# Block products for FFN2: seven instead of eight in half of the batches

## The chip, the core and the metric

The kernel runs on one core of a Trainium2 chip. A core has five engines with queues of their own: TensorE (PE: matrix products from SBUF into PSUM; its weight loads are listed as PEld), VectorE (DVE), ScalarE (ACT), GpSimd (POOL) and SyncE (SP). Each works through its own queue in order and waits only for the data, or the space, that the next instruction needs. DMA queues move data between HBM and SBUF. The metric is the device time of one execution in microseconds, lower is better.

## The reference

The inputs are q, k, v (8 batches, 8 heads, 576 tokens, 64 features), phi (the same with 32 memory slots) and four weight matrices.

```python
a = softmax(phi, axis=2)                       # over the 32 slots
k_m = einsum('bhsm,bhsd->bhmd', a, k)          # 32 slot keys per head, v_m alike
attn = softmax(q @ k_m.T / 8) @ v_m            # over the 32 slots
x = attn with the 8 heads side by side         # 4608 tokens x 512
h = max(x @ w1, x @ w2, x @ w3)                # 4608 x 768
out = h @ w_out                                # 4608 x 512, float32
```

(The softmax lines stand for an exponential divided by its sum; the reference subtracts the maximum first and adds 1e-9 to the sum.)

## The kernel before

Tokens of a batch lie so that 128 partitions hold pairs of heads. The product with v_m is never formed: x @ w = attn @ (v_m @ w), and the small v_m @ w ("fold") is made for each batch. Since max(x w1, x w2, x w3) = max(x (w1 - w3), x (w2 - w3), 0) + x w3, the hidden layer hT holds max(relu(attn wp1), attn wp2), six tiles of 128 features by the tokens of two batches, and the part x w3 w_out is added in FFN2 as attn times a folded matrix wp3 (256 slots by 512). So FFN2 of 128 tokens is eight matmuls into one PSUM bank: six hT tiles against w_out (wo_sb, L497) and two attn tiles against wp3 (L506), with 512 columns each.

The whole kernel is an order written out by hand at its end: a list of pieces, `letter number @ batch`, issued one after another. Each piece puts its instructions into the queues of its engines, so the list sets the order within every engine. A "!" moves a piece's work to the other engine (`swap`). The pieces:

- L0 to L3: load phi, k, v, q of a batch (L93, L97, L110), all from GpSimd's queue. Buffers: two batches of each. H and Y: the same for batch 0 and the weights.
- E: exponential of phi on ScalarE. r0, r1: GpSimd packs k and v into one tile kvr (`pack`, L103), from batch 2 on.
- B: the slot keys and values, 72 small matmuls over the packed k, v and a column of ones (`att_kv`, L249). N: their division by the sums on VectorE. K: transposes on TensorE and a copy. Q0, Q1: transposes of q on VectorE (`att_q`, L313).
- S: the scores and their exponential (`att_score`, L333 and L342). a, s, c: VectorE transposes, sums over the slots, reciprocals. m: the product with the reciprocals, on GpSimd (`att_mul`, L409). X: transposed back into attn (L417).
- D0 to D3: folds of v_m into w1, w2, w3 w_out (`fold`, L440, copied out at L172 or L176). F0 to F11: FFN1, one tile of features for one of the two weight differences (`ffn1`, L466); the even ones are copied with a relu (L170), the odd ones are joined by a maximum on VectorE (L479).
- T0 to T4: FFN2, 128 tokens each (`ffn2`, L497, L506). A batch of 576 tokens has four tiles of 128 and 64 tokens over; T4 of an odd batch joins the two remainders (L515). The copy from PSUM is on ScalarE for nearly all of them (L172), and SyncE writes the tile out (L527). T3 of batch 7, the last piece, is done in two halves of 256 columns (`ffn2_last`, L538, L546) with the copies on VectorE (L555) and ScalarE (L558).
- W, O, V: once, at the start: w3 transposed (into w3T), w3 w_out, and the differences w1 - w3, w2 - w3 (`w_diff`, L213). Z: warm-up matmuls.

PSUM has eight banks. A second string, `banks`, gives the bank of every piece in the order of issue; F, S, B and D take a pair, T and K one.

## Time and profile before

| | us |
|---|---|
| median of 3 timed runs | 164.94 (164.56 to 165.78) |
| span of the profiled execution, first to last instruction | 163.3 |
| end of its last matmul | 159.6 |
| TensorE busy | 153.8 (94%) |
| ScalarE busy | 100.6 (62%) |
| VectorE busy | 90.4 (55%) |
| GpSimd busy, issuing of DMAs included | 69.5 (43%) |

"Busy" is the time in which at least one instruction of the engine runs. A matmul's row gives its time from start to modelled end, which overlaps with the next; what a stream of matmuls costs is read from the distances of their starts, or from the chain that ended last. The page cuts the span into 40 slices of 4.08 us and gives busy shares as digits (9 is 90% or more). In a group's row come the line, engine and operation, the tiles written and read, their shapes and the count; behind the first bar the busy time and the mean of one in ns; behind the second the engine's idle time ahead of it and what ended most of that.

### The profile page before, as it was taken

To read this page: it belongs to the slowest core of one execution; us is meant where nothing else is said; L and a number is where in the kernel's file an instruction comes from. 1 tells how busy PE (TensorE), PEld (TensorE's weight loads), DVE (VectorE), ACT (ScalarE), POOL (GpSimd) and SP (SyncE) were. 2 spreads that over 40 slices of the span, in tenths; PEclk is the share of its full clock that TensorE was granted. 3 is DMA by queue.
4 is the path that set the end of the run, shared out by engine and by line. 5 is a ranking of instruction groups with operands and counts; after the bars stand their busy time and mean duration, and the time that the engine had idled before them with its cause. 6 is when DMAs were issued, how large, how long until landed. Compare 5 with 4: busy or idle time off the path is not lost.

```text
span 163.3 us, 4838 instructions
## 1 busy us (share of the span) xinstructions
PE 153.8 (94%) x2080; PEld 85.3 (52%) x2080; DVE 90.4 (55%) x181; ACT 100.6 (62%) x151; POOL 69.5 (43%) x71
## 2 busy tenths in 40 slices
PE   7978798899899999999999999999999999999990
PEld 2433444564377436743673575576553468744450
DVE  2023704798838665849399748879749128810010
ACT  4205445845497488778885899994658976223320
POOL 7932205100599259657968957646403100000000
PEclk9999999999999999999999999999999999999998
DMA  6999999999999999999999999996313130014333
GB/s 150 152 206 207 205 210 217 274 208 210 253 313 238 209 253 379 274 210 293 252 263 206 232 355 264 191 233 150 130 69 129 69 128 0 0 68 186 135 128 130
DMA packets 21974, 31.77 MB, mean 195 GB/s; under 512 B 1216, under 2 KB 16576, under 8 KB 21952
## 3 DMA queue, kind: packets, MB, share of 16 engines
q0 software_dynamic: 16080, 21.43, 68.7%
q1 hardware_dynamic: 5728, 9.90, 17.2%
q8 instruction: 16, 0.26, 0.6%
q10 hardware_dynamic: 144, 0.13, 0.2%
q14 instruction: 6, 0.05, 0.1%
HBM read 39.32 MB, written 9.44 MB: 299 GB/s over the span
## 4 chain that ended last, share of the span: by engine, by line
PE 83%; DMA 9%; POOL 2%; ACT 2%; issue 1%; DVE 1%; ACTq 0%; POOLq 0%
PE psum L497 29%; PE psum L466 28%; DMA wo_sb<-in_moe_w_out_dram 9%; PE psum L506 8%; PE psum L440 6%; PE psum L249 4%; PE psum L192 3%; PE psum L333 2%; PE psum L515 1%; ACT h L170 1%; PE psum L538 1%; PE psum L298 1%; POOL kvo L97 1%; ACT wp L172 1%; POOL qq L110 0%
## 5 line engine op out<-in xcount | busy, mean ns | idle before, releaser
L497 PE MATMUL psum<-wo_sb,hT 128*128 128x512 bf16 x210 | 51.3, 380 | 0.0
L466 PE MATMUL psum<-attn,wp 128*128 128x288 bf16 x384 | 50.5, 286 | 0.1
L479 DVE TENSOR_TENSOR hT<-psum,h 128x576 bf16<-128x576 f32 x48 | 34.2, 749 | 18.0 <-PE psum L466 12.5
L466 PEld LDWEIGHTS <-wp 128*128 128x128 bf16 x384 | 36.7, 98 | 13.2 <-issue 2.0
L172 ACT COPY ot<-psum 128x512 f32<-128x512 f32 x35 | 20.7, 591 | 32.1 <-PE psum L506 25.2
L497 PEld LDWEIGHTS <-hT 128*128 128x128 bf16 x210 | 19.2, 97 | 24.0 <-issue 4.3
L172 ACT CAST wp<-psum 128x1024 bf16<-128x1024 f32 (+1 forms) x31 | 29.2, 995 | 3.8 <-PE psum L440 2.0
L103 POOL COPY kvr<-kvo 128x2304 bf16<-128x2304 bf16 x12 | 25.3, 2111 | 13.7 <-DMA kvo<-in_k_dram 10.1
L170 ACT ACTIVATE h<-psum 128x576 bf16<-128x576 f32 x47 | 28.4, 659 | 3.5 <-PE psum L466 3.3
L409 POOL TENSOR_TENSOR t<-t,sm 128x576 bf16<-128x576 bf16 x14 | 16.1, 1154 | 24.6 <-DVE sm L404 24.4
L506 PE MATMUL psum<-wp,attn 128*128 128x512 bf16 x62 | 18.4, 379 | 0.0
L159 PE MATMUL psum<-warm 128*128 128x512 bf16 x44 | 12.1, 427 | 1.2 <-DVE warm L128 1.2
L313 DVE STREAM_TRANSPOSE qT<-qq 128x576 f32<-128x576 f32 x16 | 11.7, 747 | 1.4 <-DMA qq<-in_q_dram 1.4
L342 ACT ACTIVATE e<-psum 128x576 bf16<-128x576 f32 x16 | 9.6, 652 | 3.8 <-PE psum L333 3.8
L229 ACT ACTIVATE e<-ph 128x1152 bf16<-128x1152 f32 (+1 forms) x9 | 9.6, 1065 | 1.7 <-DMA ph<-in_phi_dram 1.6
L395 DVE TENSOR_REDUCE sm<-t 128x18 f32<-128x576 bf16 x14 | 10.3, 738 | 0.2
L387 DVE STREAM_TRANSPOSE t<-e 128x288 f32<-128x288 f32 x14 | 6.4, 465 | 6.2 <-ACT e L342 6.1
L97 POOL DMA_DIRECT2D kvo<-in_v_dram x9 | 6.7, 749 | 7.1 <-PE psum L249 4.1
L506 PEld LDWEIGHTS <-attn 128*128 128x128 bf16 x62 | 6.1, 98 | 7.1
L110 POOL DMA_DIRECT2D qq<-in_q_dram x8 | 6.2, 770 | 6.6 <-DVE h L174 3.7
L555 DVE COPY ot<-psum 128x256 f32<-128x256 f32 x1 | 0.4, 425 | 15.4 <-PE psum L546 15.4
L249 PEld LDWEIGHTS <-e 64*32 64x32 bf16 x720 | 6.9, 90 | 3.7 <-issue 3.3
(57 smaller groups left out, 114.4 us busy)
## 6 DMA issues: line engine op xcount, KB each, us to landing
out_dram<-ot SPq DMA_DIRECT2D x35, 256.0 KB, 5.6
qq<-in_q_dram POOLq DMA_DIRECT2D x8, 576.0 KB, 12.2
ph<-in_phi_dram POOLq DMA_DIRECT2D x7, 576.0 KB, 14.4
kvo<-in_k_dram POOLq DMA_DIRECT2D x7, 576.0 KB, 14.6
kvo<-in_v_dram POOLq DMA_DIRECT2D x7, 576.0 KB, 15.6
w_sb<-in_moe_w_dram POOLq DMA_DIRECT2D x3, 768.0 KB, 19.0
wo_sb<-in_moe_w_out_dram POOLq DMA_DIRECT2D x1, 768.0 KB, 14.6
ph<-in_phi_dram SPq DMA_DIRECT2D x2, 288.0 KB, 3.0
```

What stands on the lines that cost most here:

```text
L103: nc.gpsimd.tensor_copy(out=kvrs[b % 2][:, :, :, D * i : D * (i + 1)], in_=kvos[b % 2][:, 1 - i])
L159: nc.tensor.matmul(po[:, 0:BANK], lhsT=warm[:, 0:P], rhs=warm, start=True, stop=True)
L170: nc.scalar.activation(out=out_, in_=in_, func=AF.Relu)
L172: nc.scalar.copy(out=out_, in_=in_)
L249: nc.tensor.matmul(kvp[M * j : M * (j + 1), a, 0:nd], lhsT=s["e"][r, j, c, :], rhs={None: lambda: kvr[r, j, c, 0:nd], 0: lambda: k_and_one ...
L313: nc.vector.transpose(out=s["qT"][:, j].rearrange("p j c r e -> p (j c r e)").bitcast(FP32), in_=loaded[b]["q"][:, j].rearrange("p j c d - ...
L395: nc.vector.tensor_reduce(out=sm, in_=s["t", g].rearrange("p n r e -> p n e r"), op=ALU.add, axis=mybir.AxisListType.X,)
L409: nc.gpsimd.tensor_tensor(out=t, in0=t, in1=s["sm", g].unsqueeze(2).to_broadcast([P, S // HP, R, 2]), op=ALU.mult,)
L466: nc.tensor.matmul(acc[:, h, 0:SH], lhsT=wps[b][:, g, w * DF + ft * P : w * DF + (ft + 1) * P], rhs=attn[:, g, c0 : c0 + SH], start=(g == ...
L479: nc.vector.tensor_tensor(out=hT[:, ft, (b % 2) * S : (b % 2 + 1) * S].rearrange("p (h n) -> p h n", h=2), in0=a, in1=s["h1", ft], op=ALU.max,
L497: nc.tensor.matmul(po, lhsT=hT[:, fc, c0 : c0 + P], rhs=wo_sb[:, fc, :], start=(n == 0), stop=False,)
L506: nc.tensor.matmul(po, lhsT=attn[:, g, c0 : c0 + P], rhs=wp3s[b][:, g, :], start=False, stop=(g == NG - 1),)
```

## The change

FFN2 of batches 3, 4, 5 and 6 (512 of their 576 tokens; the 64 left over stay in T4) is done by seven products of half blocks instead of eight. The product of tokens by 1024 "features" (six hT and two attn tiles) and of 1024 by 512 is cut into two by two blocks each: tokens in two interleaved halves of 256 (r), features in two halves (three hT tiles and one attn tile each), output columns in two halves of 256. Sums and differences of blocks are formed first:

- U0 to U3: of the weights. For w_out once (batch number 9), 768 elements a partition each, on GpSimd, into the space of w3T; for wp3 of each batch, 256 elements each.
- A0 to A3: of the hT blocks, 768 elements each; A4 to A7: of the attn blocks, 256 each. A2 overwrites the block of hT it reads.
- P0 to P6: the products, eight matmuls of 256 columns each. They share three banks a batch: x for P1, P4, P5, P6, y for P0 and P3, z for P2. Partial sums are copied out of a bank while it goes on accumulating (after P0, P1 and P4); three additions on VectorE and one copy give the output, which is written out after P4 and P6, 512 KB each.

A and U run on GpSimd or VectorE according to "!" (U!: VectorE; A!: GpSimd). Five softmax products m (m1@1, m1@2, m0@2, m1@3, m1@4) go to VectorE. The list of pieces and the bank string are new, opool has four buffers instead of six, and for batches 0 and 1 the tile with k and v begins with the ones, which lie ahead of k and v now. The bank string is left out below.

```diff
-    opool = ctx.enter_context(tc.tile_pool(name="opool", bufs=6))
+    opool = ctx.enter_context(tc.tile_pool(name="opool", bufs=4))
-    def att_mul(b, g):
+    def att_mul(b, g, swap):
-        nc.gpsimd.tensor_tensor(
+        (nc.vector if swap else nc.gpsimd).tensor_tensor(
...
+    KT = FT // 2
+    CH = DM // 2
+    TW = 2 * P
+    SUB, ADD = ALU.subtract, ALU.add
+    B11, B12, B21, B22 = [
+        (slice(KT * i, KT * (i + 1)), slice(CH * j, CH * (j + 1)))
+        for i in range(2)
+        for j in range(2)
+    ]
+    tw = w3T.rearrange("p f j n -> p (f j n)").rearrange("p (i k c) -> p i k c", i=4, k=KT)
+    sa0 = const.tile([P, 4, TW], BF16, name="sa0")
+    oj0 = [const.tile([P, 2, DM], FP32, name=f"oj{i}") for i in range(2)]
+    SNAP = {0: "m5", 1: "m1", 4: "u2"}
+    twb, sas, quads = {}, {}, {}
+    def combine(on_dve, out_, in0, in1, op):
+        eng = nc.vector if on_dve else nc.gpsimd
+        eng.tensor_tensor(out=out_, in0=in0, in1=in1, op=op)
+    def combine_w(b, i, on_dve):
+        if b == B + 1:
+            x = {n: wo_sb[:, n[0], n[1]] for n in (B11, B12, B21, B22)}
+            t = [tw[:, n] for n in range(4)]
+        else:
+            if b not in twb:
+                twb[b] = work.tile([P, 4, CH], BF16, name="twb")
+            w = wp3s[b]
+            x = {n: w[:, n[0].start // KT, n[1]] for n in (B11, B12, B21, B22)}
+            t = [twb[b][:, n] for n in range(4)]
+        in0, in1 = [(x[B12], x[B11]), (x[B22], t[0]), (x[B22], x[B12]), (x[B21], t[1])][i]
+        combine(on_dve, t[i], in0, in1, SUB)
+    def sums(b):
+        if b not in sas:
+            if b == B - 1:
+                s = inp.tile([P, NP, NC, D], BF16, name="sx", tag="qq")
+                s = s.rearrange("p j c d -> p (j c d)").rearrange("p (i n) -> p i n", i=3)
+                sa = inp.tile([P, NP, NC, D], BF16, name="sy", tag="qq")
+                sa = sa.rearrange("p j c d -> p (j c d)")[:, 0 : 4 * TW]
+                sa = sa.rearrange("p (i n) -> p i n", i=4)
+            else:
+                s, sa = w_sb[:, 0:3, 2], sa0
+            sas[b] = (
+                s.rearrange("p i (k q n) -> p i k q n", k=KT, q=2),
+                sa.rearrange("p i (q n) -> p i q n", q=2),
+            )
+        return sas[b]
+    def blocks(x, b, k):
+        c0 = (b % 2) * (S + HP)
+        x = x[:, :, c0 : c0 + 2 * TW]
+        return [
+            [
+                x[:, k * i : k * (i + 1)].rearrange("p f (q r n) -> p f q r n", q=2, r=2)[
+                    :, :, :, r
+                ]
+                for i in range(2)
+            ]
+            for r in range(2)
+        ]
+    def combine_a(b, i, on_dve):
+        s, sa = sums(b)
+        n = i % 4
+        if i < 4:
+            (a11, a12), (a21, a22) = blocks(hts[b // 2], b, KT)
+            t = {0: s[:, 0], 1: s[:, 1], 2: a21, 3: s[:, 2]}
+        else:
+            (a11, a12), (a21, a22) = blocks(attns[b // 2], b, 1)
+            t = {m: sa[:, m : m + 1] for m in range(4)}
+        in0, in1 = [(a21, a22), (t[0], a11), (a11, a21), (a12, t[1])][n]
+        combine(on_dve, t[n], in0, in1, ADD if n == 0 else SUB)
+    def products(b, i, swap):
+        s, sa = sums(b)
+        h, a = blocks(hts[b // 2], b, KT), blocks(attns[b // 2], b, 1)
+        wp3 = wp3s[b]
+        def plain(r, c):
+            return lambda k, q: h[r][c][:, k, q] if k < KT else a[r][c][:, 0, q]
+        def summed(n):
+            src = h[1][0] if n == 2 else s[:, min(n, 2)]
+            return lambda k, q: src[:, k, q] if k < KT else sa[:, n, q]
+        def w_plain(i, j):
+            c = slice(CH * j, CH * (j + 1))
+            return lambda k: wo_sb[:, KT * i + k, c] if k < KT else wp3[:, i, c]
+        def w_summed(n):
+            return lambda k: tw[:, n, k] if k < KT else twb[b][:, n]
+        lhs, rhs, name = [
+            (summed(0), w_summed(0), "y"),
+            (plain(0, 0), w_plain(0, 0), "x"),
+            (plain(0, 1), w_plain(1, 0), "z"),
+            (summed(3), w_plain(1, 1), "y"),
+            (summed(1), w_summed(1), "x"),
+            (summed(2), w_summed(2), "x"),
+            (plain(1, 1), w_summed(3), "x"),
+        ][i]
+        acc = quads.setdefault(b, {})
+        if i < 3:
+            acc[name] = one_bank()
+        po = acc[name]
+        for k in range(KT + 1):
+            for q in range(2):
+                nc.tensor.matmul(
+                    po[:, q * CH : (q + 1) * CH],
+                    lhsT=lhs(k, q),
+                    rhs=rhs(k),
+                    start=(i < 3 and k == 0 and q == 0),
+                    stop=(k == KT and q == 1),
+                    skip_group_check=True,
+                )
+        x = po.rearrange("p (q n) -> p q n", q=2)
+        def copy(out_, in_):
+            if swap:
+                nc.vector.tensor_copy(out=out_, in_=in_)
+            else:
+                nc.scalar.copy(out=out_, in_=in_)
+        if i in SNAP:
+            t = ln if i == 0 else work.tile([P, S], FP32, name="snap", tag="r")
+            t = acc[SNAP[i]] = t[:, 0:DM].rearrange("p (q n) -> p q n", q=2)
+            copy(t, x)
+        if i == 2:
+            if b == B - 1:
+                ot = [inp.tile([P, NP, NC, M], FP32, name=f"ox{n}", tag="ph") for n in range(2)]
+                acc["ot"] = [
+                    x.rearrange("p j c m -> p (j c m)")[:, 0 : 2 * DM].rearrange(
+                        "p (q n) -> p q n", q=2
+                    )
+                    for x in ot
+                ]
+            else:
+                acc["ot"] = oj0
+        if i not in (2, 4, 5, 6):
+            return
+        ot = acc["ot"][i // 5][:, :, slice(0, CH) if i in (2, 6) else slice(CH, DM)]
+        if i == 6:
+            copy(ot, x)
+        else:
+            if i == 4:
+                x = acc["y"].rearrange("p (q n) -> p q n", q=2)
+            y = acc[{2: "m1", 4: "u2", 5: "m5"}[i]]
+            nc.vector.tensor_tensor(out=ot, in0=x, in1=y, op=ADD)
+        if i in (4, 6):
+            r0 = b * S + (b % 2) * HP
+            rows = out[r0 : r0 + 2 * TW].rearrange("(q r p) c -> p q r c", q=2, r=2)
+            nc.sync.dma_start(out=rows[:, :, i // 5], in_=acc["ot"][i // 5])
...
+            "U": lambda: combine_w(b, i, swap),
+            "A": lambda: combine_a(b, i, not swap),
+            "P": lambda: products(b, i, swap),
...
     for w in """
+        E@0 H2@0 H0@0 L3@0 Z25@0 B0@0 Y2@0 I@0 N0@0 Z2@0 K0@0! Q0@0 Q1@0 Z9@0 S@0 Z2@0
+        M0@0 M1@0 R0@0 R1@0 W0@0 Y3@0 W1@0 W2@0 Z6@0 O1@0 H3@0 O3@0 O2@0 H1@0 X1@0 B1@0
+        X0@0 N1@0 K1@0 O0@0 Y0@0 D1@0! D0@0! D3@0 F8@0 F10@0 F2@0 V0@0 F6@0 F0@0! Y1@0
+        D2@0 D4@0 F4@0 L0@1 V1@0 F1@0 E@1 F3@0 L1@1 F5@0 F9@0 F7@0 L3@1 U2@9 F11@0 B0@1
+        T0@0! N0@1 Q1@1 Q0@1 V2@0 K0@1! T3@0! S@1 a0@1 s0@1 L2@1 B1@1 L2@2 U0@9 T1@0
+        N1@1 c0@1 a1@1 K1@1 U1@9 s1@1 c1@1 L1@2 L0@2 m0@1 D0@1 D1@1! m1@1! X0@1 D2@1
+        X1@1 T2@0 F0@1 F10@1! F4@1 F1@1 L0@3 F11@1 L3@2 r0@2 F8@1 F5@1 L2@3 F2@1 E@2
+        F9@1 F3@1 F6@1 F7@1 D3@1 r1@2 E@3 B@2 N@2 T0@1! Q0@2 K@2 Q1@2 T2@1 L1@3 S@2
+        T4@1! a0@2 s0@2 a1@2 c0@2 D2@2 L3@3 L0@4 D0@2 T1@1 r1@3 m0@2! s1@2 c1@2 m1@2!
+        X0@2 D1@2! L1@4 X1@2 D3@2 r0@3 B@3 N@3 T3@1 F2@2 L2@4 U3@9 L3@4 Q0@3 Q1@3 K@3
+        F4@2 F10@2 F5@2 S@3 F11@2 F3@2 a1@3 F0@2 F6@2 a0@3 F7@2 F8@2 L2@5 L0@5 F1@2 F9@2
+        E@4 L1@5 D3@3 D0@3 s0@3 c0@3 r0@4 s1@3 T2@2! U0@3! D1@3! L3@5 c1@3 m1@3! r1@4
+        L0@6 m0@3 X0@3 B@4 D2@3 X1@3 U2@3 N@4 T0@2! L2@6 F6@3 A4@3! Q1@4 Q0@4 F8@3 F9@3
+        K@4! F4@3 L1@6 F10@3 r1@5 F5@3 L2@7 E@5 F11@3 F7@3 F2@3 F0@3 F3@3 r0@5 S@4 F1@3
+        D0@4 B@5 L3@6 a0@4 N@5 Q0@5 D3@4 A5@3! s0@4 Q1@5 a1@4 T1@2 K@5! A0@3! c0@4 T4@3!
+        s1@4 A1@3 L1@7 c1@4 U1@3 D1@5! S@5 U3@3 m0@4 A3@3 m1@4! A2@3! T3@2 a1@5 D2@4
+        a0@5 A6@3! A7@3 U0@4! D1@4! r1@6 X0@4 X1@4 s0@5 r0@6 D2@5 s1@5 P0@3 c0@5 r1@7
+        c1@5 U1@4 P1@3 P2@3 m0@5 L0@7 F0@4 F1@4 P3@3! E@6 P4@3! D3@5 D0@5 m1@5 B@6 L3@7
+        N@6 P5@3 F2@4 Q1@6 F4@4 K@6! F3@4 F10@4 Q0@6 A4@4! F8@4 P6@3! X0@5 S@6 r0@7 F5@4
+        F6@4 X1@5 F11@4 F7@4 F4@5 F9@4 F0@5 F10@5 A5@4 a0@6 F5@5 A0@4 F6@5 A6@4! A1@4!
+        A3@4! F7@5 F2@5 a1@6 E@7 F11@5 F3@5 s1@6 P0@4 D0@6 B@7 D2@6 U2@4 A7@4! P1@4
+        A2@4! c1@6 N@7 F1@5 P2@4! Q1@7 Q0@7 U0@5 K@7! s0@6 A4@5 F8@5 m1@6 P3@4! P4@4
+        U3@4 S@7 F9@5 c0@6 P5@4 D1@6 m0@6 D0@7 X1@6 A0@5! D3@6 a0@7 a1@7 T4@5! s0@7
+        A5@5! D1@7! c0@7 D2@7 X0@6 A1@5 D3@7! A7@5! P6@4 s1@7 P0@5 F0@6 m0@7 U1@5 c1@7
+        U2@6! F6@6 P1@5! A3@5! F8@6 m1@7 X0@7 F7@6 P2@5! U2@5 X1@7 A6@5 A4@6 P3@5! F1@6
+        A2@5! F2@6 F10@6 P4@5 U3@5 F4@6 U0@6 F6@7 P5@5! F3@6 F9@6 F11@6 P6@5! F10@7 F5@6
+        F2@7 A0@6 A5@6! F8@7 U1@6! F0@7 A7@6! F4@7! F11@7 F3@7 P0@6 A1@6 A6@6 F7@7 A3@6!
+        P1@6 F1@7 P2@6 F5@7 F9@7 A2@6 U3@6! P3@6! P4@6! T4@7! P5@6! T2@7 T1@7! T0@7!
+        P6@6 T3@7
```

## Prediction

> **What bounds the kernel now.** I read the page's head first, then the timeline of TensorE, the chain that ended last, GpSimd's timeline, and the groups by line.
>
> ```profile
> span 163.3 us, 4838 instructions
> ...
> PE   7978798899899999999999999999999999999990
> ...
> PEclk9999999999999999999999999999999999999998
> DMA  6999999999999999999999999996313130014333
> ```
>
> From the fifteenth slice on, TensorE is busy 9 tenths or more in every slice at the full granted clock. But the DMA row is full as well, up to slice 28 (114 us). Both have to be kept in view: TensorE has no gaps, and the inputs stream in without a pause until two thirds of the run are over.
>
> The chain near its end (start us, length us, what) gives the price of FFN2's matmuls when nothing disturbs them:
>
> ```profile
> 154.16 1.29 PE psum L497 x6
> 155.45 0.43 PE psum L506 x2
> ...
> 158.71 0.66 PE psum L538 x6
> 159.37 0.23 PE psum L546 x2
> ```
>
> One tile of 128 tokens is 6 + 2 matmuls of 512 columns: 1.72 us, or 215 ns each. The last tile is done in halves of 256 columns: 8 matmuls in 0.89 us, or 111 ns each. So halving the columns halves the time almost exactly.
>
> GpSimd's timeline shows when inputs arrive, because the packing copy (L103) of a batch waits for them (start us, length us; idle before it and what ended it in brackets), and TensorE's shows when the packed tiles are used:
>
> ```profile
> 83.07 2.11 POOL L103 COPY kvr<-kvo 128x2304 bf16<-128x2304 bf16 x1 [1.78 <-DMA kvo<-in_k_dram]
> 87.36 2.11 POOL L103 COPY kvr<-kvo 128x2304 bf16<-128x2304 bf16 x1 [0.74 <-DMA kvo<-in_v_dram]
> 98.05 2.11 POOL L103 COPY kvr<-kvo 128x2304 bf16<-128x2304 bf16 x1 [1.81 <-DMA kvo<-in_k_dram]
> 108.46 2.10 POOL L103 COPY kvr<-kvo 128x2304 bf16<-128x2304 bf16 x1 [3.58 <-DMA kvo<-in_k_dram]
> ```
> ```profile
> 91.29 0.83 PE L249 MATMUL psum<-kvr,e 64*32 64x129 bf16 x72
> 108.05 0.49 PE L333 MATMUL psum<-qT,kvt 32*32 32x288 bf16 x32
> ```
>
> Batch 5's k lands at 83.0, its v at 87.3; the second copy ends at 89.5, and B@5 (L249) starts at 91.3. The margin is under 2 us. So the order before is paced by two things at once, TensorE's own work and the landing of the loads.
>
> **TensorE: what the products save.** Removed are 16 tiles of FFN2 (T0 to T3 of batches 3 to 6), 16 x 1.72 = 27.5 us. Added are 28 products of 8 matmuls with 256 columns, 28 x 0.89 = 24.9 us. The saving is 2.6 us; by the step from tile to tile in the chain (eight tiles from 142.07 to 155.88, 1.73 each) it is 2.7, which I take. It is real only where TensorE never waits, so 1.7% of the span is the most the change can bring; 1% (1.6 us) is about what a measurement of this kernel can tell from no change.
>
> The Trainium skill, page "TensorE: Matmul & The Clock Gate", section "Back-to-back issue gap", gives 81 ns for a sustained pair of weight load and matmul at 128 columns and 131 ns at 512. On a line between them 256 columns would cost about 98 ns (an estimate from that page), and the change would cost TensorE 56 x 98 - 32 x 131 = 1.3 us more per batch. The trace disagrees with 215 and 111 ns, and the measurement decides.
>
> **The other engines, by rows of the page and of its groups.** The rows:
>
> ```profile
> L479 DVE TENSOR_TENSOR hT<-psum,h 128x576 bf16<-128x576 f32 x48 | 34.2, 749 | 18.0 <-PE psum L466 12.5
> L172 ACT COPY ot<-psum 128x512 f32<-128x512 f32 x35 | 20.7, 591 | 32.1 <-PE psum L506 25.2
> L409 POOL TENSOR_TENSOR t<-t,sm 128x576 bf16<-128x576 bf16 x14 | 16.1, 1154 | 24.6 <-DVE sm L404 24.4
> ```
> ```profile
> L213 DVE TENSOR_TENSOR w_sb<-w_sb 128x2048 bf16<-128x2048 bf16 x2 | 2.4, 1198 | 0.0
> L213 DVE TENSOR_TENSOR w_sb<-w_sb 128x1024 bf16<-128x1024 bf16 x2 | 1.3, 684 | 0.0
> ```
>
> - Additions of two bf16 tiles on VectorE: the two L213 forms give 0.17 us + 0.50 ns an element, so 0.56 us for 768 elements and 0.30 for 256. Seven of the first and eleven of the second: 7.2 us.
> - The same on GpSimd: no such row. L409 is the nearest (2.0 ns an element, with a broadcast): 1.54 and 0.51 us. The packing copy, one input, 0.92 ns an element, is the lower bound: 0.70 and 0.23. I take L409's. Thirteen large (four of them for w_out, once) and 21 small: 30.7 us, or 14 at the lower bound.
> - Five softmax products move: GpSimd loses 5 x 1.15 = 5.8 us. VectorE gains about 5 x 0.75 (the row of the elementwise product of the same size, L377, 0.75): 3.8.
> - PSUM: 36 tile copies become 20 copies of T, 16 of partial products and 12 additions on VectorE. ScalarE loses 10 copies net (26 of them against 36), 5.9 us by L172. VectorE gets 12 additions and 10 copies at about 0.69 (L479's 749 ns scaled from 576 to 512): 15.2.
>
> On VectorE, which is busy 90.4 us before, that is about 26 us more, 116 in all. GpSimd goes from 69.5 to about 94. By itself this fits under 160 us. In the stretch between the scores of batch 3 and of batch 7 (72.2 to 121.0 before, 48.8 us), the same sums raise VectorE from 36.6 to about 45.5 and GpSimd from 32.5 to about 48. Both are then nearly as full as TensorE; ScalarE (37.9) gets no worse. The cover is thin there, and gone where a pack waits for a load.
>
> **Waits inside a product.** P3 adds onto P0's bank after P0's copy, with P1 and P2 (1.8 us) between; P4 waits for P1's copy behind P2 and P3. P5 and P6 wait for the copy and the addition in front of them, with folds, B or F pieces or T tiles between (1.1 us or more in batch 3, 1.8 in batch 6). A copy or addition is 0.6 to 0.7 us, so I cost these at nothing; uncovered, each is about 0.8 us.
>
> **The early part.** U2@9 writes into w3T's space and stands ahead of the load L2@1 in GpSimd's queue. It must wait for the last use of w3T (26.4 in the chain), so that load goes out at about 28 instead of 19.9, and the loads behind it follow. The transfers issued earlier last until 37.7 (q of batch 1, issued at 16.1 and landed 21.6 us later), so I cost the delay at nothing. If the queue ran dry it would be up to 8 us.
>
> **The new order against the loads: the step that decides.** Ahead of B@5 in TensorE's order the new list leaves out T1@2, T3@2, T0@3, T4@3 and D1, D2, D3 of batch 4, and adds nothing: 3 x 1.73 + 1.84 (T4, with its four half-width pairs) + 3 x 0.22 (a fold of eight matmuls in the chain) = 7.7 us. TensorE would reach B@5 at 91.3 - 7.7 = 83.6. But the same loads must land first as before (k, v, q and phi of batches 1 to 4, and batch 5's phi, k and v, only in another order), through DMA engines that are already full. They landed at 87.3. What can make it earlier is that fewer output tiles are written by then, 11 against 14 or 15. From 37.7 to 114.6 us, 19 large loads, 6 of half the bytes and some 20 output tiles landed. Early loads with no outputs beside them took 2.9 us each, so an output costs about (76.9 - 22 x 2.9) / 20 = 0.66 us, and three are 2.0 us. Landing 85.3, pack 87.4, B@5 at 87.5: **a new wait of 3.9 us**.
>
> A second point gives the same. Ahead of the scores S@6 the list leaves out 9 F (0.49 us each in the chain) and 4 T, 11.3 us, and adds 7 P (6.2): 108.05 - 5.1 = 103.0. q of batch 6 landed at 104.7 before; now v of batch 7 is in front of it and phi of 7 behind: 104.7 + 1.45 - 0.7 (one output fewer) = 105.4, and two transposes (0.75 each) give 106.9, 3.9 later. The two points do not add: work behind the first is shifted by it. TensorE's later work is a fixed sum, so the shift stays to the end.
>
> **The sum**, against the profiled execution: last matmul at 159.6, - 2.7 saved, + 3.9 waited = 160.8. For the thin cover on VectorE and GpSimd I add 0.7, half the time of one GpSimd product, as one wait that reaches TensorE. The tail behind the last matmul (3.7 us) stays: span 165.2. The median of the timed runs lies 1.6 above the span (164.94 to 163.3). Predicted: **166.8 us**.
>
> **Rivals.**
> - *The loads keep up* (other side). If batch 5's second load lands by 81.4 or q of 6 by 101.5, TensorE never waits: 164.9 - 2.7 = 162.2. The point from which it decides is a wait below 2.7 us. For it: the orders before have margins of 1 to 3 us at every batch, with three loads outstanding. Against: the DMA row without a gap. Chance 0.27 to be faster by over 1%; with part of the wait within 1%, 0.24.
> - *VectorE and GpSimd get in each other's way.* Nothing before runs a two-input VectorE operation in SBUF beside GpSimd arithmetic, so it is not shown; bounds are nothing and a full wait per operation. Some ten such operations lie between the scores of 3 and of 7; at half a GpSimd operation (0.6) each VectorE goes to 51.5 us of a stretch of about 50, and 3 to 5 us reach TensorE: 170 to 171. Chance 0.15, within slower.
> - *The change is what it says, but the banks are short:* two or three single banks held for a whole group of products leave fewer pairs for F, whose pair is refilled after about 1.4 us. Price 0.1 to 0.2 us for each of some 48 F pieces: 4 to 8 at most, 169 typical. Chance 0.08.
>
> The Trainium skill, page "SBUF — State Buffer", section "Who interferes with whom", says that a VectorE instruction with two SBUF inputs contends with a GpSimd instruction that reads SBUF, and that the later one blocks fully. That is the second rival; no run here shows it yet.
>
> **Chances and range.** Slower by over 1% 0.49 (the pace of the loads with or without the rivals), within 1% 0.24, faster 0.27. The range reaches from just below the clean saving, 161.8, to 171.0.
>
> **What would show it.** Right: TensorE idle before B@5 or S@6 with the packs ending just before; DMA full until about 114 us; P matmuls at about 110 ns; last tail unchanged. Wrong: no idle of TensorE between 60 and 110 us (the first rival), L2@5 or L1@5 landing well before 85, additions on VectorE far above 0.56 us (the second), or F pieces waiting for their banks (the third).

## The result: 4% slower, not 1%

The changed kernel takes 171.62 us (170.88 to 172.67, four runs) beside 164.91 for the kernel before on the same chip: ratio 1.0394, 95% interval 1.0341 to 1.0446. The forecast was 166.8 with a range of 161.8 to 171.0. The direction was right and the size was not: 4.8 us more were lost than forecast, and the median lies above the range. Here and below, medians, ratios and intervals leave out the few runs that were over 1.5% longer than the fastest of the same kernel.

The head of the page after (busy times; then the busy tenths of TensorE, the granted clock and the DMA row in 40 slices):

```profile
span 170.4 us, 5059 instructions
...
PE 153.0 (90%) x2162; PEld 96.1 (56%) x2176; DVE 127.7 (75%) x225; ACT 95.4 (56%) x142; POOL 101.5 (60%) x100
...
PE   7977789599899999988979948999999999999992
...
PEclk9999999999999999999999996999999999999999
DMA  5999999999999999999999999695003221400536
```

TensorE's busy time fell only from 153.8 to 153.0. Where the row of before had nines from slice 12 on, there is now a 4 in slice 24 (98 to 102 us), and in the slice behind it (102 to 106 us) the clock row has a 6. VectorE and GpSimd are busier than reckoned: 127.7 and 101.5 us against 116 and 94.

TensorE's timeline at the places of the forecast (start us, length us; idle before it and what ended it in brackets):

```profile
88.41 0.80 PE L250 MATMUL psum<-kvr,e 64*32 64x129 bf16 x72 [1.09 <-POOL kvr L108]
...
102.73 1.51 PE L468 MATMUL psum<-attn,wp 128*128 128x288 bf16 x8 [2.89 <-DVE attn L419]
104.03 1.49 PE L600 MATMUL psum<-wo_sb,w_sb 128*128 128x256 bf16 x6
...
112.99 0.49 PE L335 MATMUL psum<-qT,kvt 32*32 32x288 bf16 x32
```

B@5 (first line) starts at 88.4, after a wait that a pack ended; the forecast had 87.5. The load that this pack needs, k of batch 5, landed at 86.13 (17.8 us after its issue at 68.38), and the pack began at 86.24. S@6 (last line) starts at 113.0, where the forecast had 106.9. Between them lie 2.89 us of idle time, ended by VectorE's transposes into attn, and right behind it the row of six matmuls of a product has 1.49 us instead of 0.82, as the same rows have at 97 to 99 us: from 103 to 108 us the mean granted clock was 0.66, and 1.00 on both sides.

VectorE and GpSimd ahead of that idle time:

```profile
94.00 1.33 DVE L505 TENSOR_TENSOR w_sb<-hT,w_sb 128x768 bf16<-128x768 bf16 x1
95.26 2.19 DVE L411 TENSOR_TENSOR t<-t,sm 128x576 bf16<-128x576 bf16 x1
...
98.13 2.05 DVE L505 TENSOR_TENSOR sa<-attn,sa 128x256 bf16<-128x256 bf16 x1
100.10 2.19 DVE L505 TENSOR_TENSOR twb<-wp 128x256 bf16<-128x256 bf16 x1
102.21 0.82 DVE L419 STREAM_TRANSPOSE attn<-t 128x288 f32<-128x288 f32 x2
```
```profile
94.88 1.95 POOL L505 TENSOR_TENSOR hT<-hT 128x768 bf16<-128x768 bf16 x1
96.80 1.19 POOL L505 TENSOR_TENSOR sa<-attn 128x256 bf16<-128x256 bf16 x1
97.93 6.32 POOL L108 COPY kvr<-kvo 128x2304 bf16<-128x2304 bf16 x3
```

Two sums of 256 elements (A7@3, U0@4), reckoned at 0.30 us each, take 2.05 and 2.19 us on VectorE, each about as long as the packing copy (2.1 us) that runs beside it, and each ending 0.14 us behind that copy. The product m1@4 takes 2.19 instead of 0.75, beside the sum A2@3 on GpSimd (94.88). The transposes that TensorE waits for stand behind them in VectorE's queue. The same operations without GpSimd arithmetic beside them are as reckoned, by the groups (the last number ahead of the second bar is the mean of one in ns):

```profile
L505 DVE TENSOR_TENSOR twb<-wp 128x256 bf16<-128x256 bf16 x3 | 5.0, 1657 | 0.0
L505 DVE TENSOR_TENSOR twb<-wp,twb 128x256 bf16<-128x256 bf16 x2 | 0.6, 284 | 0.0
L411 DVE TENSOR_TENSOR t<-t,sm 128x576 bf16<-128x576 bf16 x5 | 7.4, 1488 | 0.1
L216 DVE TENSOR_TENSOR w_sb<-w_sb 128x2048 bf16<-128x2048 bf16 x2 | 4.9, 2468 | 0.0
```

The last row is the early part: V, 1198 ns before, is 2468 now. One of the two takes 3.75 us (at 28.29), until 1.09 us behind the end of U0@9 on GpSimd (29.29 to 30.95). U1@9, the next sum there, takes 2.50 us instead of 1.64, so each engine holds the other. TensorE waits 1.30 us for what is behind V, and S@1 starts at 41.4 instead of 39.5.

The products themselves and the tail cost what was forecast; the chain near its end:

```profile
163.94 0.43 PE psum L666 x2
164.37 0.87 PE psum L600 x8
...
166.12 0.66 PE psum L698 x6
166.77 0.23 PE psum L706 x2
```

From S@6 to the last matmul 54.0 us pass; 51.55 + 5.1 - 2.7 = 53.95 were forecast. So nearly the whole error lies ahead of S@6.

### The profile page after: what moved, and what is told of

Read it like the earlier page. It is cut to its first block, busy times and chain, and to the rows that moved or that the text cites. A ratio compares the mean times of both kernels' runs of the same rounds, so it can differ in the third digit from the quotient of the medians.

```text
span 170.4 us, 5059 instructions
## 1 busy us (share of the span) xinstructions
PE 153.0 (90%) x2162; PEld 96.1 (56%) x2176; DVE 127.7 (75%) x225; ACT 95.4 (56%) x142; POOL 101.5 (60%) x100
## 5 line engine op out<-in xcount | busy, mean ns | idle before, releaser
L468 PE MATMUL psum<-attn,wp 128*128 128x288 bf16 x384 | 52.1, 287 | 4.5 <-DVE attn L419 2.9
L173 ACT ACTIVATE h<-psum 128x576 bf16<-128x576 f32 x45 | 27.6, 655 | 15.6 <-PE psum L468 15.5
L657 PE MATMUL psum<-wo_sb,hT 128*128 128x512 bf16 x103 | 26.4, 380 | 1.2 <-issue 1.0
L175 ACT COPY ot<-psum 128x512 f32<-128x512 f32 x14 | 8.3, 590 | 22.6 <-PE psum L666 13.4
L411 POOL TENSOR_TENSOR t<-t,sm 128x576 bf16<-128x576 bf16 x9 | 11.1, 1233 | 11.1 <-DVE sm L406 11.0
L505 POOL TENSOR_TENSOR w_sb<-hT,w_sb 128x768 bf16<-128x768 bf16 x3 | 4.9, 1639 | 8.3 <-DVE w_sb L505 8.2
L442 PE MATMUL psum<-w_sb,kvt 64*32 64x512 bf16 (+1 forms) x200 | 8.5, 373 | 0.9 <-DMA w_sb<-in_moe_w_dram 0.5
L98 POOL DMA_DIRECT2D kvo<-in_k_dram x9 | 6.9, 772 | 3.4 <-DMA qq<-in_q_dram 2.6
L666 PE MATMUL psum<-wp,attn 128*128 128x512 bf16 x30 | 8.9, 379 | 0.0
L505 POOL TENSOR_TENSOR w3T<-wo_sb 128x768 bf16<-128x768 bf16 x2 | 3.3, 1647 | 9.4 <-PE psum L195 9.4
## 6 DMA issues: line engine op xcount, KB each, us to landing
wo_sb<-in_moe_w_out_dram POOLq DMA_DIRECT2D x1, 768.0 KB, 14.6
```

The costliest lines, as they stand in the source:

```text
L173: nc.scalar.activation(out=out_, in_=in_, func=AF.Relu)
L175: nc.scalar.copy(out=out_, in_=in_)
L411: (nc.vector if swap else nc.gpsimd).tensor_tensor(out=t, in0=t, in1=s["sm", g].unsqueeze(2).to_broadcast([P, S // HP, R, 2]), op=ALU.mult,)
L468: nc.tensor.matmul(acc[:, h, 0:SH], lhsT=wps[b][:, g, w * DF + ft * P : w * DF + (ft + 1) * P], rhs=attn[:, g, c0 : c0 + SH], start=(g == ...
L657: nc.tensor.matmul(po, lhsT=hT[:, fc, c0 : c0 + P], rhs=wo_sb[:, fc, :], start=(n == 0), stop=False,)
L666: nc.tensor.matmul(po, lhsT=attn[:, g, c0 : c0 + P], rhs=wp3s[b][:, g, :], start=False, stop=(g == NG - 1),)
```

## Experiments

The theory after the result: VectorE's operations with two inputs in SBUF are **blocked** by GpSimd's arithmetic (the second rival), in the middle and in the early part, and the **loads** make TensorE wait at B@5 as forecast. The rivals: loads alone, with the sums innocent, or simply too much work on GpSimd. All ratios are to the kernel before, with 95% intervals.

**Two sums moved.** A7@3 and U0@4 go to GpSimd, nothing else changes.

```diff
-        a0@5 A6@3! A7@3 U0@4! D1@4! r1@6 X0@4 X1@4
+        a0@5 A6@3! A7@3! U0@4 D1@4! r1@6 X0@4 X1@4
```

> The changed kernel with A7 of batch 3 and U0 of batch 4 on GpSimd instead of VectorE; nothing else is edited. In the changed kernel these two took 2.05 and 2.19 us beside two packing copies (0.3 us each where GpSimd was idle), and behind them TensorE stood idle for 2.9 us and then ran about 4 us at a lower clock. Theory (VectorE's operations with two SBUF inputs and GpSimd's arithmetic block each other, and this place costs most): the idle time and the slow clock go, 4 to 5 us, so 167 us; TensorE reaches S@6 at about 108. Rival one (too much work on VectorE, not blocking): 0.6 us of work moves, so 171.0. Rival two (the landing of loads holds TensorE anyway): within 0.5 us of 171.6.

Measured: ratio 1.0211 (1.0144 to 1.0277), median 168.7. The idle time and the low clock are gone (clock 1.00 over the run), S@6 starts at 108.83; B@5 stays at 88.65. Two additions of 0.3 us each cost the changed kernel about 3 us (0.0183 of 165), and the time missed the expected 167 by 1.7.

**No sums at all.** Every A and U is left out, and the products read unsummed blocks, so that the output is another.

```diff
-            src = h[1][0] if n == 2 else s[:, min(n, 2)]
-            return lambda k, q: src[:, k, q] if k < KT else sa[:, n, q]
+            return plain(n % 2, n // 2)
...
-            return lambda k: tw[:, n, k] if k < KT else twb[b][:, n]
+            return w_plain(n // 2, n % 2)
```

> The changed kernel without any A and U (the products read unsummed blocks, so the output is not the reference's); products, copies, additions, loads and order are as in the changed kernel. Blocking theory with the pace of the loads beside it: 166 to 167 us, with B@5 still waiting for its second packing copy at about 87. If the loads do not matter and the sums are everything: 162 to 163. If short PSUM banks or the copies and additions are the cause: 169 or more.

Measured: 1.0128 (1.0054 to 1.0203), 167.4, just above the expected 166 to 167. S@1 is back at 39.5, and with nothing else in the way the wait for the pack is longer, and the pack itself waits for its load:

```profile
88.67 0.80 PE L250 MATMUL psum<-kvr,e 64*32 64x129 bf16 x72 [2.52 <-POOL kvr L108]
```
```profile
86.51 2.11 POOL L108 COPY kvr<-kvo 128x2304 bf16<-128x2304 bf16 x1 [2.45 <-DMA kvo<-in_k_dram]
```

B@5 starts at the same time as with the sums (88.41). So the loads set this point, and without the sums the kernel is still slower than before. Part of that is the clock: behind this wait the granted clock was 0.50 for 3.4 us (89.5 to 92.9), which costs about 1.7 us.

**Short loads.** For batches 3 to 7 only one of the four pairs of k and v is loaded; the rest of the buffers keeps what was in it, so the output is another. Once on the changed kernel, once on the kernel before, once without sums.

```diff
     def load_kv(b, i, h=slice(0, NP)):
+        if b > 2:
+            h = slice(0, 1)
```

> The changed kernel with a quarter of the bytes of k and v loaded for batches 3 to 7 (the output is not the reference's). If the pace of the loads costs what was forecast at B@5: B@5 at 84 to 85 instead of 88.4, and 167 to 168.5 us. If blocking alone is the cause: B@5 may come earlier but the queue behind A7@3 and U0@4 keeps its place against TensorE, within 1 us of 171.6.

> The kernel before with the same short loads of k and v for batches 3 to 7. If the loads pace the kernel before only through margins (as the profile was read): within 1 us of 164.9. If they hold it back too: 163 or less.

> The changed kernel without any A and U and with a quarter of the bytes of k and v for batches 3 to 7 (the output is not the reference's). This leaves the seven products, their copies and additions and the new order. If blocking and the pace of the loads are the two costs: no waits of TensorE of note between 40 and 130 us, and the products' own saving shows, 162 to 163 us. If the banks or the additions cost something of their own: 165 or more.

Measured: the changed kernel 1.0265 (1.0185 to 1.0345), between the two expectations, with B@5 at 86.6 where 84 to 85 was expected; the kernel before 0.9993 (0.9965 to 1.0021), so the loads cost it nothing; without sums 0.9904 (0.9868 to 0.9940), 163.8, above the expected 162 to 163. In the changed kernel with short loads B@5 has no wait for a pack (86.60), but 2.24 us of idle time behind VectorE's attn remain. With neither sums nor full loads the kernel is 1.6 us (0.0096 of 165) faster than before, where the forecast's clean saving was 2.7. All products, their banks and their copies are still in it, so the 4 to 8 us of the third rival are not there. Its largest remaining gap of TensorE in the middle is neither of the two:

```profile
69.59 0.28 PE L337 MATMUL psum<-qT,kvt 32*32 32x288 bf16 x1 [1.60 <-issue]
```

**The blocking by itself.** The kernel before, with nothing but the five products m moved to VectorE.

```diff
-        nc.gpsimd.tensor_tensor(
+        (nc.vector if swap else nc.gpsimd).tensor_tensor(
```

> The kernel before with the five softmax products on VectorE, as in the change, and nothing else. Blocking theory: those that meet GpSimd arithmetic take 1.4 to 2.2 us instead of 0.75, but VectorE has a quarter of its time free here, so 165 to 166.5 us. If VectorE's speed alone counted: 164.5 to 165 us with each at 0.75.

Measured: 1.1109 (1.1079 to 1.1138), 183.5 us. This was the largest miss: 18.4 us instead of at most 1.6. VectorE's and GpSimd's timelines at one of the five, and TensorE's behind it:

```profile
81.94 6.48 DVE L409 TENSOR_TENSOR t<-t,sm 128x576 bf16<-128x576 bf16 x1
88.46 0.48 DVE L417 STREAM_TRANSPOSE attn<-t 128x288 f32<-128x288 f32 x1
```
```profile
81.60 0.75 POOL L97 DMA_DIRECT2D kvo<-in_v_dram  x1
82.33 4.17 POOL L103 COPY kvr<-kvo 128x2304 bf16<-128x2304 bf16 x2
86.43 0.74 POOL L97 DMA_DIRECT2D kvo<-in_k_dram  x1
87.16 0.76 POOL L93 DMA_DIRECT2D ph<-in_phi_dram  x1
87.91 2.47 POOL L103 COPY kvr<-kvo 128x2304 bf16<-128x2304 bf16 x1
```
```profile
88.99 3.27 PE L466 MATMUL psum<-attn,wp 128*128 128x288 bf16 x13 [5.33 <-DVE attn L417]
```

An operation of 0.76 us stands 6.48 us, through two packs and two DMA issues without a pause between them, and TensorE stands idle for 5.33 us. The five took 3.40, 2.15, 0.76, 6.48 and 6.03 us; the 0.76 is the one with no pack beside it. Not all of the 18.4 us is waiting: behind two of the waits the granted clock was 0.50 for 6.8 and 3.4 us.

**The same with cut packs.** Each packing copy becomes four, one for each pair.

```diff
-        nc.gpsimd.tensor_copy(
-            out=kvrs[b % 2][:, :, :, D * i : D * (i + 1)], in_=kvos[b % 2][:, 1 - i]
-        )
+        for j in range(NP):
+            nc.gpsimd.tensor_copy(
+                out=kvrs[b % 2][:, j, :, D * i : D * (i + 1)], in_=kvos[b % 2][:, 1 - i, j]
+            )
```

> The kernel before with the five softmax products on VectorE and each packing copy of GpSimd cut into four (one per pair of heads). With whole copies the five took 3.40, 2.15, 0.76, 6.48 and 6.03 us, and the kernel 183.5 us. If VectorE gets its turn between two GpSimd instructions: none over about 1.5 us, and 166 to 171 us. If it waits until GpSimd's run of instructions ends: the same 6 us, and 182 to 186.

Measured: 1.0058 (1.0022 to 1.0095), 166.1 us. The packs take 30.5 us in place of 25.3, and the five products take 1.05, 0.76, 0.76, 0.89 and 0.71. VectorE and GpSimd at the place of the 6.48:

```profile
78.61 0.89 DVE L410 TENSOR_TENSOR t<-t,sm 128x576 bf16<-128x576 bf16 x1
```
```profile
78.26 0.75 POOL L97 DMA_DIRECT2D kvo<-in_v_dram  x1
78.99 2.85 POOL L104 COPY kvr<-kvo 128x576 bf16<-128x576 bf16 x4
```

More work on GpSimd, in smaller grains, won back 17 us. Two of the five stand beside packs in both kernels, and there 3.40 became 1.05 and 6.48 became 0.89; the two that took 2.15 and 6.03 no longer meet a pack. At the places that can be compared it is the length of GpSimd's instructions that VectorE pays for, not their sum.

**No products m on VectorE**, on top of the two moved sums: the five go back to GpSimd (m1@1! becomes m1@1, and so on).

> The changed kernel with A7 of batch 3 and U0 of batch 4 on GpSimd, and the five softmax products back on GpSimd too, so that VectorE keeps only ten or so sums in the middle. In the changed kernel the five took 0.76, 0.76, 1.58, 2.15 and 2.19 us on VectorE. If what is left of blocking costs time: 166.5 to 168 us against 168.7 with the two sums alone moved. If GpSimd's own work (5.8 us more ahead of packing copies and load issues) costs as much: 169 to 171.

Measured: 172.6 and 174.0 us, too few runs for an interval, some 5 us above the kernel with two sums moved and above both expectations. VectorE's sums are mostly free, but GpSimd's queue is later and the packs with it:

```profile
PE psum L250 <- POOL kvr L108: 6.5, 3, 3.5
```

(us that TensorE waited for packs, times, longest.) So the amount of GpSimd's work counts as well, through the packs.

**The sums of w_out later.** U2, U0 and U1 of w_out move from the early part to U3, in front of L3@4, on top of the two moved sums.

> As the run with A7 of batch 3 and U0 of batch 4 on GpSimd, and in addition the first three sums of w_out (U2, U0, U1 of number 9) stand right ahead of U3 instead of at the start, so that they no longer meet VectorE's weight differences and no longer stand ahead of loads. TensorE should reach S@1 at 39.5 instead of 41.5. If the loads pace the middle: the gain is gone by B@5 (88 us again) and the time is that of the run without this move, within 1 us. If only blocking counts: 1.5 to 2 us faster than that run.

Measured: 1.0256 (1.0222 to 1.0289), 169.2; S@1 is at 39.6, but B@4 then waits 3.2 us for its pack, and the gain of the early part is gone, as expected if the loads set the pace. Here it was not the loads, though. The load of that pack, v of batch 4, landed at 74.07, and the pack began at 76.50: the four sums of w_out in a row (64.11 to 70.80) and the four DMA issues behind them had put off GpSimd's queue.

**Two sums moved and short loads.**

> The changed kernel with A7 of batch 3 and U0 of batch 4 on GpSimd and with a quarter of the bytes of k and v for batches 3 to 7 (the output is not the reference's). Each of the two edits alone gave 168.7 and 169 to 170 us. If blocking and the pace of the loads are two costs in a row, both go: 164.5 to 166.5, with what is left of blocking at the start (about 1.5 us) still in it. If they are one cost seen twice: 168 or more.

Measured: 1.0102 (1.0048 to 1.0157), 166.8, just above the expected 164.5 to 166.5. The profile shows the next blocked place: a product m at 65.01 takes 3.66 us on VectorE, beside a pack at 65.89, and TensorE stands 2.67 us for what is behind it. That profile is of a run of 169.7 us, three above the median, so whether this place also stood in the others isn't known.

**Cut packs, cut sums, and both with short loads**, on the changed kernel. "Cut sums" makes three instructions of 256 elements out of each sum of 768 on GpSimd.

```diff
-            nc.gpsimd.tensor_copy(out=out_, in_=in_)
+            for j in range(NP):
+                nc.gpsimd.tensor_copy(out=out_[:, j], in_=in_[:, j])
...
-        eng.tensor_tensor(out=out_, in0=in0, in1=in1, op=op)
+        if on_dve or in0.shape[1] == 1 or len(in0.shape) == 2:
+            eng.tensor_tensor(out=out_, in0=in0, in1=in1, op=op)
+        else:
+            for j in range(in0.shape[1]):
+                eng.tensor_tensor(out=out_[:, j], in0=in0[:, j], in1=in1[:, j], op=op)
```

> The changed kernel with each packing copy cut into four, one per pair, as was done to the kernel before with five products on VectorE. If a VectorE operation with two SBUF inputs stays blocked for a whole run of unbroken GpSimd instructions, the sums near 98 us (2.05 and 2.19 us) fall below 1 us, the idle time of TensorE near 102.7 (2.9 us) and the slow clock behind it go, S@6 starts near 108.5 instead of 113.0, and the time is 168 to 169.5, as where two sums went to GpSimd. If the amount of GpSimd work is what counts, not its grain, nothing is won and the 5 us that the cut copies cost GpSimd come on top: 171.5 to 174.

> The same, and GpSimd's sums of 768 elements cut into three of 256 as well (U of w_out, A0 to A3). By the grain theory the weight difference V near 28 us (3.75 us beside two sums on GpSimd) falls to below 2, S@1 starts near 40 instead of 41.4; but the loads still set B@5 (88 to 88.7), so the time is that of the kernel with cut packs within 1 us. If the early delay adds to the rest, it is 1.4 lower than that kernel.

> Cut packs, and only a quarter of the bytes of k and v loaded for batches 3 to 7, so the products there work on what the buffers hold. With both causes taken away only the early 1.4 us should be left of the loss: 164.5 to 166. If something else is left over besides blocking and loads, it stays above 167.

> The changed kernel with packs and GpSimd's large sums cut, and a quarter of the bytes of k and v loaded for batches 3 to 7. If load wait, blocking in the middle and blocking in the early part make up the whole loss, S@1 starts near 39.3, S@6 near 105, and the time is 163.5 to 164.5, some 3 us below the kernel with cut packs alone and short loads (166.8), and level with the one that has no sums at all (163.8). If the extra GpSimd work of the cut instructions costs as much as the early delay, it stays at 166 or more.

Measured: cut packs 1.0300 (1.0235 to 1.0365), 170.5; with cut sums 1.0201 (1.0154 to 1.0249), 168.8; cut packs and short loads 1.0080 (1.0053 to 1.0107), 166.8; all three 0.9921 (0.9892 to 0.9950), 163.9. The two sums of 2.05 and 2.19 us, with cut packs:

```profile
100.14 0.61 DVE L506 TENSOR_TENSOR sa<-attn,sa 128x256 bf16<-128x256 bf16 x1
100.67 0.74 DVE L506 TENSOR_TENSOR twb<-wp 128x256 bf16<-128x256 bf16 x1
```

and V of 3.75 us, with cut packs and sums:

```profile
28.05 1.47 DVE L217 TENSOR_TENSOR w_sb<-w_sb 128x2048 bf16<-128x2048 bf16 x1
```

In all three the wait fell when the GpSimd instruction beside it was cut. The product m1@4 is a check on this: with cut packs alone it stood beside a whole sum and still took 2.19 us, and with the sums cut as well it took 1.22. By time, cut packs alone did less than the expected 168 to 169.5 (the intervals of 1.030 and 1.039 overlap). GpSimd worked 106.3 us in place of 101.5, and the blocked V was still there. With the sums cut as well the median was 1.7 us lower, so the early delay adds to the rest. Cut packs with short loads came out between its two expectations, all three inside the expected 163.5 to 164.5. The starts on TensorE in one profile of each kernel (us):

| kernel | S@1 | B@5 | B@5 to B@6 | last matmul ends | ratio |
|---|---|---|---|---|---|
| changed | 41.4 | 88.4 | 19.4 | 167.0 | 1.039 |
| two sums moved | 41.5 | 88.7 | 15.0 | 162.8 | 1.021 |
| cut packs | 41.9 | 88.6 | 16.8 | 164.9 | 1.030 |
| cut packs and sums | 39.1 | 87.1 | 16.2 | 162.9 | 1.020 |
| no sums | 39.5 | 88.7 | 15.7 | 163.1 | 1.013 |
| short loads | 41.9 | 86.6 | 17.4 | 163.3 | 1.027 |
| cut packs, short loads | 42.4 | 87.2 | 15.2 | 161.7 | 1.008 |
| cut all, short loads | 40.9 | 85.2 | 14.6 | 158.8 | 0.992 |
| no sums, short loads | 40.3 | 86.1 | 14.1 | 158.9 | 0.990 |

The column B@5 to B@6 shows the blocking in the middle most of all (19.4 with it, 15.0 with only two sums moved, 14.1 to 14.6 in the last row and the one above it), B@5 the loads. Neither is clean: short loads alone bring 19.4 to 17.4, cut packs at full loads leave 16.2 to 16.8, and the 15.7 without sums holds the 3.4 us at half the clock. With both causes gone the kernel with all its sums is level with the one that has none, so no further cost of the sums shows. The causes do not add. In ratios times 165 us, cutting alone wins 3.2, short loads alone 2.1, both 7.8. The likely reason is that while TensorE stands for one cause, the other catches up unseen.

**Products where nothing else runs.** If the sums must not meet packs and the order must not outrun the loads, the products belong behind the last pack. The order of the kernel before is kept, and T0 to T3 of batches 6 and 7 become products in the tail. In the first version the P0 sums of both batches were copied into one buffer, so that the second overwrote the first and the output is another; in the second batch 7 has a space of its own (a freed tile of k and v), the sums of w_out come after m1@6, T3@5 stands ahead of the first sums as cover, and T4@7 comes last.

```diff
-... F1@6 F3@7 T0@6! T0@7! T3@5 T2@7! T2@6! T1@6 T1@7 T3@6 T4@7! T3@7
+... F1@6 F3@7 T3@5 A0@6 A1@6 A3@6 P1@6 P2@6 A0@7 A1@7 P1@7 P2@7 A3@7 A2@6 A2@7 P0@6 P0@7 P3@6
+P3@7 P4@6 P4@7 P5@6 P5@7 P6@6! P6@7 T4@7
```

> A version meant to beat both: the order before up to the last maxima, and then batches 6 and 7 (not 3 to 6) by seven products, so that they lie behind all loads and packing copies. The sums of weights go to GpSimd after its last other work, the sums of hT and attn to VectorE after that, so that no two-input operation of VectorE meets GpSimd arithmetic. Eight tiles at 1.73 us become fourteen products at 0.89: 1.4 us less, 163.5 us, if the additions keep up. If the copies and additions between products hold TensorE, or the 512 KB writes end late: 165 to 167.

> The version with batches 6 and 7 by products behind the order before, with its tail mended after what the first one showed (waits of 0.7 us for the last maximum, 1.1 us for a sum, 0.7 us for copies and additions, and partial sums of the two batches in one buffer). The sums of w_out go to GpSimd between its last products, the sums of attn too, so that VectorE has only A0 to A3 in the tail; T3 of batch 5 stands first behind the maxima as cover, T4 of batch 7 comes last in two halves. The last matmul should end at 158.3 instead of 159.6, so 163.6 us. If the additions between P4, P5 and P6 still hold TensorE, or the late 512 KB writes end last: 164.5 to 166.

Measured: the first 1.0106 (1.0090 to 1.0123), 166.9, with waits of TensorE of 0.71 for hT and 1.10 for a sum; the second 0.9968 (0.9939 to 0.9997), 164.55 against 165.11 in twelve runs and seventeen. Its sums on VectorE are free:

```profile
144.56 0.55 DVE L505 TENSOR_TENSOR w_sb<-hT 128x768 bf16<-128x768 bf16 x1
145.14 0.56 DVE L505 TENSOR_TENSOR w_sb<-w_sb,hT 128x768 bf16<-128x768 bf16 x1
145.73 0.56 DVE L505 TENSOR_TENSOR w_sb<-hT,w_sb 128x768 bf16<-128x768 bf16 x1
```

It beats the kernel before by half a microsecond, where 1.3 was expected, and the interval only just leaves out no change.

## Why the prediction was right in direction and too small

- **The wait for the loads at B@5: right.** Landing forecast at 85.3, measured at 86.1; B@5 forecast at 87.5, measured at 88.4, and 85.2 to 87.2 in the four kernels of the table with short loads. It is the forecast's likeliest case, and short loads are worth 4.6 us by ratio once nothing is blocked, and 3.7 without sums, where some 1.7 of it is the slow clock behind the wait; 3.9 were forecast. Its unhindered start was too early, 83.6 reckoned and 85.2 measured at best, and in the changed kernel TensorE stood only 1.09 us there, with 0.16 and 1.05 at the two packs before, because it arrived late.
- **"For the thin cover on VectorE and GpSimd I add 0.7": the step that failed.** In place of 0.7 the stretch from B@5 to B@6 lost 4.4 us by the kernel with two sums moved (19.4 against 15.0), and some 5 against the kernels with neither cause (14.1 and 14.6): 2.89 us idle and the slow clock behind it. The forecast knew the mechanism as its second rival, priced it at 3 to 5 us, gave it 0.15 and left it out of the sum. The price held. It should have been a term of the sum: A7@3 and U0@4 stand in the list right ahead of r1@6 and r0@6, each 2.11 us long, and a full wait for each was the upper bound that the forecast itself had named.
- **What it missed in that rival:** the price of one block. It took half a GpSimd operation, 0.6 us; the blocked operations waited up to a whole pack, and in the kernel before with five products for several in a row. About 1.7 us of the loss came on top, from the low clock behind the idle time (0.66 in the mean over 5 us): two products took 1.6 to 1.7 us each in place of 0.87. The kernel with two sums moved has neither.
- **The early part "costed at nothing": wrong, by 1.9 us at S@1,** though not for the reason that was weighed (a late load). V was blocked by U0@9; with the early sums cut or left out S@1 lies at 39.1 to 40.9, otherwise at 41.4 to 42.4 (in the 42.4, cut packs with short loads, is a stretch of 3.4 us at half the clock, from 33.0). By the time of the whole kernel it counts only where the loads do not take it back.
- **The five products m on VectorE, "VectorE gains 3.8": off by half.** They took 7.4 us; by themselves on the kernel before they cost 18.4. Yet in this kernel they can't simply go back, since GpSimd then packs too late.
- **The saving of 2.7: half right.** Matmul by matmul it holds (0.87 us for a product, 1.72 for a tile, 54.0 us from S@6 to the end), but the two kernels with both causes gone win only 1.3 and 1.6. The rest is lost ahead of B@5, which the two reach at 85.2 and 86.1 instead of 83.6. In one of the two profiles 1.6 us of it is the gap of TensorE's own issue; what makes that gap, and what the rest is, is not settled.
- **GpSimd's 30.7 us for sums: a little low.** 256 elements took 0.67 us and 768 took 1.64, for 0.51 and 1.54; the total is 101.5 in place of 94.
- Waits inside a product and the banks, costed at nothing: right, as far as the profile of the changed kernel shows. The one large wait beside a product was VectorE's.

That VectorE stops is what the Trainium skill states, page "SBUF — State Buffer", section "Who interferes with whom": an operation of VectorE with two SBUF inputs and a GpSimd instruction that reads SBUF exclude each other, and the later one stands until the other is done. This case's traces agree (sums of 0.28 us took 2.05 and 2.19, each ending 0.14 us behind the pack beside it), and transposes with one input show nothing of it: in the kernel with five m moved the transposes into attn took 420 to 479 ns, one of them beside a pack (88.46). That the later one stands holds where GpSimd was idle when VectorE began. In the changed kernel a product m then took its 0.76 us, and it was the pack that took longer, 2.54 us instead of 2.11:

```profile
61.11 0.76 DVE L411 TENSOR_TENSOR t<-t,sm 128x576 bf16<-128x576 bf16 x1
```
```profile
61.30 2.54 POOL L108 COPY kvr<-kvo 128x2304 bf16<-128x2304 bf16 x1 [0.66 <-DMA kvo<-in_k_dram]
```

It does not hold by the listed starts where GpSimd was issuing DMAs with arithmetic right behind them: V began 1.0 us ahead of the sum on GpSimd and still took 3.75 us.

## What to carry to other kernels

When an edit puts a two-input operation with both inputs in SBUF on VectorE, look at what GpSimd runs at that moment, and price each at the whole GpSimd instruction beside it, as a term of the sum and not as a rival. If GpSimd has long copies, cut them: with pieces of 0.68 us five moved products cost 1 us, with copies of 2.11 us they had cost 18. And two causes of waiting that lie near each other hide each other, so judge a fix with the other cause taken away as well.

## What the runs showed of the hardware

- A blocked VectorE operation can stay blocked beyond one instruction: 6.48 and 6.03 us for 0.76, across two packs and the DMA issues ahead of or behind them. In the second case it began at 103.93, 1.2 us before the pack (105.15), while GpSimd issued DMAs. The issue alone does not hold VectorE: in the changed kernel a product m beside two issues (at 45.76), with an idle gap of 0.49 us before the next pack, took 0.76, and so it is in all 24 cases of these profiles with no arithmetic right behind the issue. With arithmetic right behind it one took 2.15 us (at 77.55, the product on GpSimd at 77.91). How far ahead of its start the arithmetic holds VectorE is open: 0.90 us ahead of a pack a product m took 0.76 us (short loads, 65.20), 0.88 us ahead 3.66 (two sums moved and short loads, 65.01).
- A pack cut into four costs GpSimd 0.68 us a piece, 2.7 for 2.11.
- After 2.89 us of idle time TensorE's granted clock was 0.66 in the mean over the next 5 us, and products took twice their time. After 2.52 us (no sums) and 3.24 us (sums of w_out later) it was 0.50 for 3.4 us; after 5.33 us, in the kernel before with five m moved, it was 0.73 over 88 to 100 us. After 2.24 us, in the changed kernel with short loads, and after 2.65 us, with no m on VectorE, it stayed at 1.00, so the length of the wait alone does not decide. Where the clock falls for 3.4 us, the wait costs about 1.7 us more than its length here.
- TensorE's rows of products overlap: a matmul of 256 columns is listed with 273 ns and issued every 109 (0.87 us for eight in the chain).
